# A planner's constant for one exponential, and how open feed-forward chains are completed before the last output tiles, in a fused attention and feed-forward kernel

## The chip, the cores and the metric

The kernel runs on one core of a Trainium2 chip. The metric is the device time of one execution in microseconds, less is better; the median of several runs is compared. The core has five engines with a queue each: TensorE (PE in the profile, its weight loads as PEld), VectorE (DVE), ScalarE (ACT), GpSimd (POOL) and SyncE (SP). Each works through its own list in order and waits on semaphores for the others.

## The reference

Input x has 2048 rows of 512 numbers. Two branches are computed from it and mixed by a gate for each row, all in bfloat16:

```python
g = sigmoid((x * gate_w).sum(-1, keepdims=True))
qkv = (x @ wqkv) -> q, k, v, 32 heads of 16 numbers     # a: attention
p = softmax(q @ k^T * 16 ** -0.5)                       # 32 x 2048 x 2048
a = (p @ v, heads put side by side) @ wo
b = (silu(x @ w_gate) * (x @ w_up)) @ w_down            # b: feed-forward, F = 1792
out = g * a + (1 - g) * b
```

The softmax has 32 x 2048 x 2048 exponentials, 134 million. That is the large part of the elementwise work.

## The kernel before

**Tiling.** The queries are cut into 4 blocks of 512 (qb), the heads into 8 groups of 4 (g). A unit is one (qb, g); there are 32. A unit walks over 16 tiles of 128 keys, so there are 512 slots (SLOTS), each of 4 score blocks of 128 keys x 512 queries, one for each head.

**Two ways to an exponential.** Most slots go to ScalarE: `emit_pair` puts two score blocks side by side into one PSUM tile s_t (two of them exist), and one activation writes their exponentials to e_t, 128 x 1024. The other slots go to VectorE: `emit_d` puts a score block into d_t, one of three single PSUM banks, and VectorE works out the exponential bit by bit: a first pass y_t<-d_t for each of four blocks, then passes over the whole 128 x 2048 tile (z_t by bit masks, a scaling to u_t, its square, a product with z_t), an addition that an accumulating DMA on GpSimd's queue does, and a last pass y_t<-y_t. The buffer u_t is at times a part of kaug or wd_t, and the profile then names that. `v_unit` and `v_take` decide when VectorE takes another slot, from the end of a unit backwards: it takes one when VectorE's clock in the plan leaves room and the unit's ScalarE work would not be done sooner.

**What else runs.** The probabilities are multiplied with v into o_ps (`emit_pv`), which a cast takes to osb. Beside it run the projections (kp, qp, vp), the feed-forward work, and the output. Feed-forward work comes in chains of small pieces: for each qb 14 gate/up chains (gu_a, gu_b, 8 pieces each: two matmuls a piece, then a tanh th on ScalarE and two VectorE steps gs and mt), then two down chains (dps_a, dps_b, 28 pieces each), whose results VectorE scales into bblk. The output rows of an earlier qb are made by chains a_ps. For the last qb a chain `last_pieces` of 10 pieces makes the products of the first two row tiles (a_l_a, a_l_b) without the last head group, and `tail` makes those of the other two (al).

**What sets the order.** The order of each engine's instructions is written out by a planner that runs when the program is built. It keeps clocks `plan.pe`, `plan.dve` and `plan.act` and adds fixed costs to them: 0.216 us for a matmul step, 0.6 to 1.135 us for the passes of VectorE, 0.48 us for a tanh, and ACT_US = 0.935 us for an exponential of 128 x 1024. Between two score pairs TensorE gets side work for as long as the next s_t tile is not free by these clocks:

```python
        room = s_end[pairs[0] % 2] - plan.pe      # s_end: the planned end of the exponential that frees s_t
```

`fill_dve` hands VectorE's list out up to `plan.pe`. A Pacer chooses among the chains by deadline, and deadlines are slots, not microseconds. A chain can have chains before it (`after`) and a condition (`cond`); `force(c)` puts out what is left of a chain at once, its predecessors first, and pays the VectorE work that it is owed (`owed` is the list of VectorE and other steps that are put off until their inputs are ready). The cost that the planner takes for the ScalarE part of what is left of a unit is another constant, TILE_US = 1.87, which stays.

**The end.** When all exponentials are placed, a loop places the last products with v. With one of them left it calls `tail(0)`, which places the first half of the al products; then come the last product with v, the cast to osb, the rest of al (`tail(1)`), the denominators of the last head group (dt, rt, rps), on_l, one matmul for each of four row tiles, the gate's factor, and the output. `tail(0)` needs bblk scaled for all four row tiles (`scaled`) and the head group before the last one normalised (`here_done`).

Of the kernel before, what the change touches and what calls it, by code (L numbers as in the profile page):

```python
# [78 lines left out]
def kernel(  # L79
# [76 lines left out]
    def mm(*args, **kw):  # L156
        return ordered(nc.tensor.matmul(*args, **kw))  # L157

    def act(*args, **kw):
        ordered(nc.scalar.activation(*args, **kw))  # L160
# [88 lines left out]
    for h in range(8):  # L249
        c = 2 * (h % 4) + h // 4  # L250
# [33 lines left out]
    owed = []  # L284
# [19 lines left out]
    def spend_v(cost, ready=0.0, key=None):  # L304

        if key is not None and key == plan.last:
            cost += 0.13
        plan.last = key
        plan.dve = max(plan.dve, ready) + cost

    def pay(i=0):
        ready, cost, f, c, key = owed.pop(i)
        spend_v(cost, ready, key)
        keep, plan.chain = plan.chain, None
        f()
        plan.chain = keep
        if c is not None:
            c.owed -= 1
            if c.done():
                c.done_at = plan.slot  # L320
# [27 lines left out]
    def emit_piece(c):  # L348
        mms, f = c.pieces[c.i][:2]
        c.i += 1  # L350
        keep, plan.chain = plan.chain, c
        f()
        plan.chain = keep
        if c.done():
            c.done_at = plan.slot
        return mms

    def force(c):
        for a in c.after:
            force(a)  # L360
        while not c.out():
            while c.cond is not None and not c.cond():
                if owed:
                    pay()
                else:
                    for f in at.pop(min(at)):
                        f()
            emit_piece(c)
        while c.owed:
            pay()  # L370
# [282 lines left out]
    def down_pieces(qb, tq):  # L653

        def rows(t):
            return lambda fc: (mt[:, fc, t * P:(t + 1) * P], wd_t[:, fc, :])

        def done_down(pa, pb):
            for t, p in ((tq, pa), (tq + 1, pb)):
                later(0.65, lambda t=t, p=p: end(t, p))  # L660

        def end(t, p):
            n = qb * TQ + t
            share = omg if qb < QB - 1 else ge
            vec.tensor_scalar(out=bblk[:, t, :], in0=p[:, 0:D], scalar1=share[:, n:n + 1],
                              scalar2=None, op0=ALU.mult)
            if qb == QB - 1:
                scaled.add(t)
            m_free(p, plan.dve)
        return two_banks(FC, "dps", rows(tq), rows(tq + 1), done_down)  # L670
# [27 lines left out]
    def emit_pair(bs):  # L698
# [10 lines left out]
        def exp():  # L709
            act(out=e_t[:], in_=s_t[:], func=ACT.Exp, scale=inv_sqrt_dh)  # L710
            plan.act = max(plan.act, ready) + ACT_US
            s_end[i] = plan.act + 0.2
# [5 lines left out]
        pairs[0] += 1  # L718

    exps = []  # L720
    ACT_US = 0.935

    def flush_act(before=None):

# [203 lines left out]
    def last_rows(t):  # L928
        cs = slice(t * P, (t + 1) * P)
        return lambda i: ((onc[QB - 1][:, i, cs], wo_t[:, i, :]) if i < NB - 1 else  # L930
                          (osbs[UNITS - 2][:, cs], wo_l[:, 0, :]) if i == NB - 1 else (ident[:, :], bblk[:, t, :]))
# [7 lines left out]
    def tail(k):  # L939

        if k == 0:
            assert here_done and len(scaled) == TQ
            for c in list(pace.chains):
                force(c)
            al = ps_s.tile([P, 2 * QBW], F32, tag="s", name="al")
            a_ps.extend([al[:, 0:QBW], al[:, QBW:2 * QBW]])
        todo = [(tq, i) for tq in (2, 3) for i in range(NB + 1)]
        for tq, i in todo[:5] if k == 0 else todo[5:]:
            w, r = last_rows(tq)(i)
            mm(a_ps[tq][:, 0:D], lhsT=w, rhs=r, start=(i == 0), stop=False)  # L950
# [86 lines left out]
    pace = Pacer()  # L1037
# [52 lines left out]
    for qb in range(QB):  # L1090
        a0 = f0 + per * qb
        for fc in range(FC):
# [12 lines left out]
            c = pace.add(pcs, 58, a0 + per * (0.6 if qb < QB - 1 else 0.68) * (fc + 1) / FC, prev)  # L1105
            prev = [c]
        for tq in range(0, TQ, 2):
            c = pace.add(down_pieces(qb, tq), 0 if qb else 100, a0 + per * (0.6 + 0.3 * (tq + 2) / TQ if qb < QB - 1 else 0.68 + 0.32 * (tq + 2) / TQ), prev + fin_prev + gates)
# [105 lines left out]
    def side(most):  # L1214

        due = any(not c.out() for n in range(plan.slot, plan.slot + 12) for c in need.get(n, []))
        cur = pace.cur
        begun = cur is not None and not cur.out() and cur.i and pace.credit > -3
        c = pick() if pace.credit > 0 or due or begun else None
        if c is None:  # L1220
            return None
        mms, _, takes = c.pieces[c.i][:3]
        mode, two = c.pieces[c.i][3:] or ("F", None)
        if two and two["seq"] == plan.seq:
            return None
        t = m_ready(int(takes)) if takes else 0.0
        if t is None or t > plan.pe or 0.226 * mms + (0.1 if plan.mode != mode else 0.0) > most:
            return None
        return c
# [70 lines left out]
    while au < UNITS:  # L1300
# [10 lines left out]
        if room > 0.02:  # L1311
# [6 lines left out]
            c = side(room + SLACK)  # L1318
# [26 lines left out]
    while closed < UNITS or vops or added or vcur:  # L1345
        fill_dve()
        while owed and owed[0][0] <= plan.pe:
            pay()
        if plan.slot < SLOTS + 1:
            begin(plan.slot + 1)  # L1350
            pace.credit = max(pace.credit, 2.0)
        if vcur:
            emit_d()
            continue
        c = side(2.0)
        if not pv_list(plan.pe) and c is not None:
            put_piece(c)
            continue
        if closed == UNITS - 1 and pvs[closed] == KT - 1:
            tail(0)  # L1360
        next_pv()
# [13 lines left out]
    un = UNITS - 1  # L1375
    osb = osbs[un]
    tail(1)
    dt = m_tile("dt")
    for tq in range(TQ):
# [54 lines left out]
```

## Time and profile before

| | |
|---|---|
| median of 4 runs | 844.99 us (843.76 to 846.82) |
| profiled execution | 845.75 us, span of the trace 844.0 us |
| mean granted TensorE clock | 0.996 |
| busy: PE, DVE, ACT, POOL | 91%, 94%, 97%, 11% of the span |
| exponentials on ScalarE (e_t) | 846, busy 792.4 us |
| slots on VectorE (z_t) | 89 |
| tanh (th) | 56, busy 37.9 us |

The span goes from the first to the last instruction of the trace; the execution's own time holds 1.75 us more. A group's line reads: kernel line, engine, operation, output<-input by the program's names, sizes, count | busy us, mean ns of one | idle time of the engine ahead of it, and what ended that. Line 160 is the helper through which all activations go, 157 that of the matmuls, 166 that of VectorE's instructions, so groups are told apart by their tiles. A wait's line reads: who waited <- who released it: us in total, times, longest. Neighbouring instructions of one engine overlap a little, so the mean duration of one is longer than the step from one start to the next.

### The profile page before, as it was taken

What the parts mean: (1) busy time and instruction counts of PE and PEld (TensorE: products, weight loads), DVE (VectorE), ACT (ScalarE), POOL (GpSimd) and SP (SyncE); (2) the same over time, 40 slices, a digit from 0 to 9 for tenths busy, and PEclk for the clock granted to TensorE, in tenths of its full rate; (3) what the DMA queues carried; (4) which work ended last, traced back from release to release, by engine and by line L of the source; (5) the groups of instructions that cost most, each with busy time, mean ns of one, the idle gap of its engine ahead of it and who ended that gap; (6) DMA issues with size and microseconds to landing.
All of it is one profiled execution on the core that took longest, in us unless ns stands there. A gap on an engine that the chain in (4) does not pass through costs nothing.

```text
span 844.0 us, 16253 instructions
## 1 busy us (share of the span) xinstructions
PE 769.0 (91%) x6076; PEld 263.5 (31%) x6076; DVE 796.6 (94%) x1159; ACT 815.6 (97%) x912; POOL 93.2 (11%) x122
## 2 busy tenths in 40 slices
PE   7999998999888998889889989899899898988997
PEld 3222233332232332222223333223333233332332
DVE  6999998999999999999999999999998999999996
ACT  3999999999999999999999999999999999999996
POOL 5010100010011011011010100100100110111000
PEclk9999999999999999999999999999999999999999
DMA  9432445345454334554444354454442454354232
GB/s 205 127 65 49 85 80 113 64 93 109 95 107 99 74 70 104 108 115 91 87 94 90 70 113 95 84 121 85 104 84 55 91 122 94 77 116 98 57 69 50
DMA packets 101415, 78.23 MB, mean 93 GB/s; under 512 B 77760, under 2 KB 89624, under 8 KB 101336
## 3 DMA queue, kind: packets, MB, share of 16 engines
q0 software_dynamic: 12672, 46.14, 28.7%
q1 hardware_dynamic: 86792, 30.60, 15.3%
q8 instruction: 47, 0.77, 0.4%
q10 hardware_dynamic: 1872, 0.46, 0.2%
q14 instruction: 32, 0.26, 0.1%
HBM read 20.83 MB, written 2.34 MB: 27 GB/s over the span
## 4 chain that ended last, share of the span: by engine, by line
DVE 25%; PE 14%; ACT 7%; issue 3%; DMA 1%; SPq 0%; DVEq 0%; ACTq 0%
DVE y_t L166 9%; ACT e_t L160 7%; DVE kaug L166 4%; PE s_t L157 4%; DVE u_t L166 4%; PE o_ps L157 2%; DVE z_t L166 2%; DVE gs L166 2%; PE dps_b L157 2%; DVE mt L166 2%; PE d_t L157 1%; PE dps_a L157 1%; PE gu_b L157 1%; PE gu_a L157 1%; DVE osb L166 1%
## 5 line engine op out<-in xcount | busy, mean ns | idle before, releaser
L160 ACT ACTIVATE e_t<-s_t 128x1024 bf16<-128x1024 f32 x846 | 792.4, 1105 | 8.8 <-PE s_t L157 7.2
L157 PE MATMUL s_t<-qx,kaug 64*128 64x512 bf16 x1376 | 294.3, 381 | 33.8 <-ACT e_t L160 29.0
L166 DVE TENSOR_SCALAR y_t<-d_t 128x512 uint16<-128x512 f32 x356 | 234.7, 682 | 16.8 <-PE d_t L157 13.7
L157 PEld LDWEIGHTS <-kaug 64*128 64x128 bf16 x2048 | 137.3, 93 | 322.5 <-issue 286.9
L157 PE MATMUL o_ps<-e_t,vaug 128*32 128x512 bf16 x1692 | 160.0, 390 | 1.4 <-DVE osb L166 1.0
L157 PE MATMUL gu_a<-xT,wg 64*128 64x512 bf16 x448 | 137.0, 380 | 0.0
L157 PE MATMUL gu_b<-xT,wu 64*128 64x512 bf16 x448 | 135.7, 380 | 1.2 <-DVE y_t L166 0.9
L157 PE MATMUL d_t<-qx,kaug 64*128 64x512 bf16 x288 | 107.5, 378 | 16.0 <-DVE y_t L166 8.5
L157 PEld LDWEIGHTS <-vaug 128*32 128x32 bf16 (+1 forms) x2132 | 45.7, 94 | 146.3 <-issue 144.8
L778 POOL DMA_DIRECT2D y_t<-u_t x44 | 40.2, 913 | 351.0 <-PE s_t L157 192.9
L778 POOL DMA_DIRECT2D y_t<-kaug x38 | 35.9, 946 | 311.7 <-PE s_t L157 161.6
L157 PE MATMUL dps_a<-wd_t,mt 64*128 64x512 bf16 x224 | 65.3, 376 | 0.0
L157 PE MATMUL dps_b<-wd_t,mt 64*128 64x512 bf16 x224 | 65.0, 376 | 0.3 <-DVE y_t L166 0.2
L166 DVE TENSOR_SCALAR z_t<-y_t 128x2048 uint16<-128x2048 uint16 x89 | 61.5, 691 | 2.1
L166 DVE TENSOR_SCALAR y_t<-y_t 128x2048 uint16<-128x2048 uint16 x89 | 60.9, 684 | 1.5 <-DMA y_t<-u_t 1.1
L166 DVE TENSOR_TENSOR u_t<-u_t 128x2048 f16<-128x2048 f16 x44 | 53.8, 1223 | 1.1
L166 DVE TENSOR_TENSOR u_t<-u_t,z_t 128x2048 f16<-128x2048 f16 x44 | 53.5, 1217 | 0.1
L157 PE MATMUL s_t<-q,kaug 64*128 64x512 bf16 x212 | 44.0, 386 | 7.6 <-ACT e_t L160 7.0
L166 DVE TENSOR_TENSOR kaug<-kaug 128x2048 f16<-128x2048 f16 x39 | 47.7, 1223 | 0.9
L157 PEld LDWEIGHTS <-wg 64*128 64x128 bf16 x448 | 41.4, 95 | 20.5 <-issue 8.5
L166 DVE TENSOR_TENSOR kaug<-kaug,z_t 128x2048 f16<-128x2048 f16 x39 | 47.5, 1217 | 0.1
L157 PEld LDWEIGHTS <-wu 64*128 64x128 bf16 x448 | 42.2, 95 | 16.6 <-issue 1.5
(131 smaller groups left out, 636.5 us busy)
## 6 DMA issues: line engine op xcount, KB each, us to landing
y_t<-u_t POOLq DMA_DIRECT2D x44, 512.0 KB, 4.8
y_t<-kaug POOLq DMA_DIRECT2D x38, 512.0 KB, 4.8
wg<-in_B_w_gate_dram SPq DMA_DIRECT2D x56, 128.0 KB
wu<-in_B_w_up_dram SPq DMA_DIRECT2D x56, 128.0 KB
y_t<-wd_t POOLq DMA_DIRECT2D x6, 512.0 KB, 4.7
on<-osb SPq DMA_DIRECT2D x120, 16.0 KB
rb<-rr SPq DMA_DIRECT2D x15, 128.0 KB
wd_t<-in_B_w_down_dram SPq DMA_DIRECT2D x7, 256.0 KB
```

What stands on the lines that cost most here:

```text
L157: return ordered(nc.tensor.matmul(*args, **kw))
L160: ordered(nc.scalar.activation(*args, **kw))
L166: return lambda *a, **kw: ordered(f(*a, **kw))
L778: nc.gpsimd.dma_start(out=ya, in_=ua, accum_op=ALU.add)
```

## The change

The planner counts 0.920 us instead of 0.935 us for an exponential. And `tail(0)` first completes all chains that are open, in the order of their deadlines, then pays all steps that are still owed, and only then makes sure of its conditions; before, it made sure of them first, and completed open chains in the order in which they were added.

```diff
@@ -718,7 +718,7 @@
         pairs[0] += 1
 
     exps = []
-    ACT_US = 0.935
+    ACT_US = 0.92
 
     def flush_act(before=None):
 
@@ -939,9 +939,11 @@
     def tail(k):
 
         if k == 0:
+            for c in sorted(pace.chains, key=lambda c: c.deadline):
+                force(c)
+            while owed:
+                pay()
             assert here_done and len(scaled) == TQ
-            for c in list(pace.chains):
-                force(c)
             al = ps_s.tile([P, 2 * QBW], F32, tag="s", name="al")
             a_ps.extend([al[:, 0:QBW], al[:, QBW:2 * QBW]])
         todo = [(tq, i) for tq in (2, 3) for i in range(NB + 1)]
```

## The prediction

> **What bounds the kernel now.** I read, in this order, the engine table and the chain of waits of the page, the list of waits, ScalarE's instructions in order of time, the groups by cost, and the last 20 us of the timeline.
>
> ```profile
> span 844.0 us, 16253 instructions
> PE 769.0 (91%) x6076; PEld 263.5 (31%) x6076; DVE 796.6 (94%) x1159; ACT 815.6 (97%) x912; POOL 93.2 (11%) x122
> ...
> DVE 25%; PE 14%; ACT 7%; issue 3%; DMA 1%; SPq 0%; DVEq 0%; ACTq 0%
> ```
>
> The table alone would name ScalarE, at 97%. The chain does not: ScalarE carries 7 points of it, VectorE 25, TensorE 14. Three engines are almost full, and the two that look less full are the ones that release the work that ended last.
>
> ```profile
> PE s_t L157 <- ACT e_t L160: 36.7, 109, 0.9
> ...
> DVE y_t L166 <- PE d_t L157: 13.7, 23, 1.0
> ...
> PE d_t L157 <- DVE y_t L166: 9.6, 21, 0.9
> ...
> ACT e_t L160 <- PE s_t L157: 7.2, 15, 1.5
> ```
>
> Here each engine waits for another. ScalarE seems to lose 7.2 us only, but a delay shorter than the overlap of two exponentials leaves no idle time in this view. Their spacing does show it. First come all exponentials, from the view of tile e_t, then two stretches of ScalarE's timeline that hold nothing but exponentials (start, length, count).
>
> ```profile
> L160 ACT ACTIVATE e_t<-s_t x846: 1018/1112/1312, 18.7 to 834.5; 128x1024 bf16<-128x1024 f32 x170
> ```
>
> ```profile
> 298.75 13.86 ACT L160 ACTIVATE e_t<-s_t 128x1024 bf16<-128x1024 f32 x15 [0.17 <-PE s_t L157]
> ...
> 815.38 20.27 ACT L160 ACTIVATE e_t<-s_t 128x1024 bf16<-128x1024 f32 x22 [0.75 <-PE s_t L157]
> ```
>
> From first start to last start is 815.8 us. The 56 tanh take 0.47 us each in this order (one starts at 312.35, the next exponential at 312.82), 26.3 us in all, so one of the 845 steps took (815.8 - 26.3) / 845 = 0.934 us. Undisturbed it takes (20.27 - 1.11) / 21 = 0.912 us, and (13.86 - 1.11) / 14 = 0.911 us. So ScalarE is kept waiting for about 845 x 0.022 = 18.6 us, most of it hidden. The kernel runs at the pace for which its instruction order was written (0.935), and ScalarE is a little faster than that. That is the room this change can use.
>
> One rule of the Trainium skill says there is no such room. The page "ScalarE: Activation LUTs", section "What ACT_TABLE_LOAD costs", gives 186 ns + 0.833 ns per element for an activation and an overlap of about 93 ns between neighbours; for 1024 elements that is an estimate of 0.946 us per exponential, and ScalarE would be the bound with nothing to recover. The 0.912 above differs, and it decides; by the page the sum would be that of the first rival below.
>
> **Part 1: 0.935 becomes 0.920.** No instruction is made faster. The number moves the planner's clock: it thinks that each of 846 exponentials ends 0.015 us earlier, 12.7 us in all. Fewer microseconds between two score pairs mean less VectorE work fits, and VectorE decides how many key tiles it takes over. One such tile costs, from the groups:
>
> ```profile
> L166 DVE TENSOR_SCALAR y_t<-d_t 128x512 uint16<-128x512 f32 x356 | 234.7, 682 | 16.8 <-PE d_t L157 13.7 <-PE s_t L157 2.0 <-PE gu_a L157 0.7
> ...
> L166 DVE TENSOR_SCALAR z_t<-y_t 128x2048 uint16<-128x2048 uint16 x89 | 61.5, 691 | 2.1
> L166 DVE TENSOR_SCALAR y_t<-y_t 128x2048 uint16<-128x2048 uint16 x89 | 60.9, 684 | 1.5 <-DMA y_t<-u_t 1.1 <-DMA y_t<-kaug 0.2
> ```
>
> To these 357.1 us come the same table's three other passes, each spread over the buffers u_t, kaug and wd_t: scaling 31.2 + 27.8 + 4.1, squares 53.8 + 47.7 + 7.3, products 53.5 + 47.5 + 7.3. That is 637.3 us for 89 tiles, 7.16 us a tile. If m tiles go back to ScalarE, the planner's time shrinks by 12.7 - 1.84 m (two exponentials a tile), and VectorE, equally full in a shorter time, must lose as much: 7.16 m = 12.7 - 1.84 m, m = 1.4. So I expect 1 or 2 tiles fewer of 89, and about 3 exponentials more than 846. With them:
> - VectorE loses 1.4 x 7.16 = 10.1 us of work.
> - ScalarE gains 2.8 x 0.934 = 2.6 us.
> - TensorE: a tile on VectorE has four score matmuls one after the other (some 0.21 us apart in the timeline), a pair for ScalarE two side by side. So it loses about 1.4 x 2 x 0.21 = 0.6 us.
> - Each lost tile takes away its accumulating transfer on POOL's queue (512 KB). POOL is busy for 11%, so I cost that at nothing; were it needed, the addition lands after 4.8 us. The weight loads on SP's queue keep their number and order; they move with the feed-forward chains, two chains ahead of use.
>
> What of it is on the path? The chain weighs the engines 25 : 14 : 7, that is 0.54, 0.30 and 0.15 of the 46 points that are engine work. -10.1 x 0.54 - 0.6 x 0.30 + 2.6 x 0.15 = -5.3 us. The ends: -10.1 if the whole shorter order comes true, +2.6 if ScalarE is the sole pace. I take -5.3, since all three engines have holes and none of them alone sets the time. What is late next is ScalarE: the shorter order and its 2.6 us of new work leave it 5.9 us of its 18.6 us (18.6 - 10.1 - 2.6) if all comes true, so holes cannot vanish much further.
>
> **Part 2: completion at the end.** The order shrinks, but the feed-forward work doesn't, and it shares PSUM banks and VectorE's evictions with everything else. So it ends later against the last exponential. Before, it just gets done:
>
> ```profile
> 827.31 0.74 DVE L166 TENSOR_SCALAR bblk<-dps_b,ge 128x512 bf16<-128x512 f32 x1
> ...
> 831.63 0.38 PE L157 MATMUL a_l_a<-bblk,ident 64*128 64x512 bf16 x1
> ...
> 833.87 0.39 PE L157 MATMUL s_t<-qx,kaug 64*128 64x512 bf16 x2 [0.53 <-ACT e_t L160]
> ...
> 835.96 0.40 PE L157 MATMUL o_ps<-e_t,vaug 128*32 128x512 bf16 x4
> 836.41 0.69 DVE L166 CAST osb<-o_ps 128x512 bf16<-128x512 f32 x1 [2.04 <-PE o_ps L157]
> ```
>
> The last down products are scaled at 827.31 to 828.05, the output pieces a_l end at 832.0, the last exponential starts at 834.5. From 831.9 to 834.8 TensorE is busy for 2.15 of 2.90 us; by start spacing it issues 3 score pairs and 3 groups of o_ps, about 6 x 0.22 = 1.3 us. So its cover is 0.75 to 1.6 us. Each quarter of the feed-forward work belongs to a quarter of the order; a quarter of 10.1 is 2.5 us of lateness, if the earlier quarters catch up. Over the cover it sticks out by 0.9 to 1.75 us. I take 1.0. In that case chains are open at the tail, and they are completed ahead of the al products and the last group of o_ps on TensorE; behind that group wait, one after the other, the osb cast, the denominators dt and rps, on_l, four output products, mt and the output's transfer (835.96 to 844.0), so each microsecond there is one of the end. On VectorE the owed scalings stand ahead of that cast. The ends of this term: 0, and 8.5 if all 10.1 us of lateness is left at the end.
>
> **Sum.** The profiled execution took 845.75 us (span 844.0 and 1.75 around it); 845.75 - 5.3 + 1.0 = 841.45. It stands 0.76 above the median of 844.99, so I forecast 840.7 for the median, -0.5%.
>
> **Rivals.** (1) *ScalarE is the pace*: the holes stay as they are, because they come from matmuls that sit in TensorE's order between two score pairs, and there are 3 exponentials more: +2.6, and the tail's 1.0. 844.99 + 3.6 = 848.6, slower. For it: 97% busy, and TensorE's longest list of waits (36.7 us) ends on ScalarE. Against it: the 0.022 us a step, and its small part in the chain. It decides from the point at which less than 1.1 us of the 18.6 us is won back (3.6 less 2.5, the 0.3% at which a measurement of this kernel can tell a change from none). (2) *The feed-forward work is the pace at the end*: about 6 us of the lateness piles up there instead of 2.5, as one chain of down products is 28 steps of two matmuls, 6 us at 0.21 each. -5.3 + 6 - 1.6 = -0.9: 844.1, within 0.3%. For it: PE is full in the last 20 us with these very steps. At over 9.4 us open (1.6 + 5.3 + 2.5) it would be slower. (3) *The constant does too little*: the order absorbs the 12.7 us in gaps that the planner leaves on TensorE and VectorE (47 us of VectorE idle in the span), no tile moves: 845.0.
>
> **How the numbers follow.** Forecast 0.52, rival 1 0.22, rival 2 0.18, rival 3 0.08. Faster by over 0.3%: 0.48 of the forecast (the rest of it is too small a gain) and 0.04 of rival 2, 0.52. Within: 0.04 + 0.10 + 0.08 = 0.22. Slower: 0.22 + 0.04 = 0.26. The range goes from the whole shorter order with nothing at the tail, 844.99 - 10.1 = 834.9, to rival 1's 848.6; the likeliest case alone has 835 to 842.5.
>
> **What would show it.** Right: 86 to 88 z_t instructions instead of 89, 848 to 852 exponentials, a mean step nearer 0.92 than 0.934, VectorE's busy time down by about 10 us, a_l pieces that end less than 1 us ahead of the last exponential or behind it, and the distance from the last exponential's start to the span's end, 9.5 us now, at 10 to 11. Wrong: a step still at 0.93 (rival 1), that last distance at over 14 us (rival 2), 89 tiles and the same order (rival 3).

## The result, and the profile after

The changed kernel takes 847.68 us (median of 47 runs), the kernel before 844.85 (71 runs): ratio 1.003, 95% interval 1.002 to 1.004. It is slower by 2.8 us; 840.7 was forecast, a gain. The profiled execution took 850.90 us with a span of 847.4.

The same parts of the page, from the changed kernel:

```profile
span 847.4 us, 16311 instructions
PE 774.3 (91%) x6104; PEld 267.0 (32%) x6104; DVE 788.6 (93%) x1149; ACT 814.8 (96%) x914; POOL 90.4 (11%) x122
...
DVE 23%; ACT 16%; PE 16%; issue 4%; DMA 2%; DVEq 0%; ACTq 0%
```

VectorE works 8.0 us less (796.6 to 788.6), and ScalarE's part in the chain goes from 7 to 16. Next the tile views of z_t and e_t (count: shortest/median/longest in ns, first to last start):

```profile
L166 DVE TENSOR_SCALAR z_t<-y_t x88: 627/693/695, 29.0 to 821.7; 128x2048 uint16<-128x2048 uint16 x88
```

```profile
L160 ACT ACTIVATE e_t<-s_t x848: 1017/1151/1315, 18.9 to 832.4; 128x1024 bf16<-128x1024 f32 x170
```

One slot went back to ScalarE, two exponentials more, and yet the last one starts at 832.4 instead of 834.5. A step is (832.40 - 18.94 - 56 x 0.47) / 847 = 0.929 us, against 0.934. So the loop became 2.1 us shorter in this execution. The end became longer: from the last exponential's start to the end of the span it is 15.0 us, against 9.6. That is +5.4 - 2.1 = +3.4 us of span (rounded), 844.0 to 847.4. The timeline of the end shows on what TensorE spends it:

```profile
834.47 0.38 PE L157 MATMUL dps_a<-wd_t,mt 64*128 64x512 bf16 x1
...
834.89 0.75 DVE L166 TENSOR_SCALAR bblk<-dps_a,ge 128x512 bf16<-128x512 f32 x1 [2.38 <-PE dps_b L157]
...
835.69 0.37 PE L157 MATMUL a_l_b<-wo_t,on 64*128 64x512 bf16 x1 [0.62 <-DVE bblk L166]
...
837.88 0.38 PE L157 MATMUL a_l_a<-bblk,ident 64*128 64x512 bf16 x1
...
839.38 0.40 PE L157 MATMUL o_ps<-e_t,vaug 128*32 128x512 bf16 x4
...
839.83 0.69 DVE L166 CAST osb<-o_ps 128x512 bf16<-128x512 f32 x1 [3.53 <-PE o_ps L157]
```

Before, the last down products were scaled at 827.31 and the a_l pieces done at 832.0, ahead of the last exponential. Now 8 steps of dps and all 10 of a_l come after it, with a wait of 0.62 us for bblk. Only behind them stand the al products and the last group of o_ps, and the cast waits 3.53 us for that group. It starts 7.0 us after the last exponential's start (839.4 - 832.4), against 1.5 before (835.96 - 834.48). The rest of the end is the same.

### The profile page after: what moved, and what is told of

It reads as the page before. It is cut to its first block, busy times and chain, and to the rows that moved or that the text cites. A ratio compares the mean times of both kernels' runs of the same rounds, so it can differ in the third digit from the quotient of the medians.

```text
span 847.4 us, 16311 instructions
## 1 busy us (share of the span) xinstructions
PE 774.3 (91%) x6104; PEld 267.0 (32%) x6104; DVE 788.6 (93%) x1149; ACT 814.8 (96%) x914; POOL 90.4 (11%) x122
## 4 chain that ended last, share of the span: by engine, by line
DVE 23%; ACT 16%; PE 16%; issue 4%; DMA 2%; DVEq 0%; ACTq 0%
ACT e_t L160 15%; DVE y_t L166 8%; PE s_t L157 5%; DVE u_t L166 4%; DVE kaug L166 4%; PE o_ps L157 3%; PE dps_a L157 2%; DVE z_t L166 2%; DVE mt L166 2%; PE d_t L157 2%; DVE gs L166 2%; ACT th L160 1%; PE dps_b L157 1%; DMA y_t<-kaug 1%; PE gu_a L157 1%
## 5 line engine op out<-in xcount | busy, mean ns | idle before, releaser
L157 PE MATMUL s_t<-qx,kaug 64*128 64x512 bf16 x1380 | 284.4, 384 | 46.8 <-ACT e_t L160 41.7
L157 PEld LDWEIGHTS <-kaug 64*128 64x128 bf16 x2048 | 141.1, 93 | 334.2 <-issue 298.8
L166 DVE TENSOR_SCALAR y_t<-d_t 128x512 uint16<-128x512 f32 x352 | 231.7, 682 | 12.3 <-PE d_t L157 10.6
L157 PE MATMUL gu_a<-xT,wg 64*128 64x512 bf16 x448 | 134.7, 376 | 0.0
L778 POOL DMA_DIRECT2D y_t<-kaug x37 | 33.5, 905 | 310.9 <-PE s_t L157 139.7
L166 DVE TENSOR_TENSOR kaug<-kaug 128x2048 f16<-128x2048 f16 x37 | 45.3, 1224 | 1.1
L166 DVE TENSOR_TENSOR kaug<-kaug,z_t 128x2048 f16<-128x2048 f16 x37 | 45.0, 1217 | 0.0
```

The costliest lines, as they stand in the source:

```text
L166: return lambda *a, **kw: ordered(f(*a, **kw))
L778: nc.gpsimd.dma_start(out=ya, in_=ua, accum_op=ALU.add)
```

## The experiments

Theory A: the loop wins, and the open feed-forward work at the end takes more than that. Theory B: ScalarE is the pace, and its additional exponentials are the loss. The first four runs separate them; later ones are on other constants and on the clock. All times are medians, and each ratio is to the kernel before in the same call, whose median went from 844.65 to 845.31. "Half clock" is how long TensorE's granted clock was 0.5 before the last exponential, in the profiled execution.

| run | constant | what else | exponentials | last one starts | from there to the end | half clock | time, us | ratio to before (95%) |
|---|---|---|---|---|---|---|---|---|
| before | 0.935 | | 846 | 834.5 | 9.6 | 6.8 | 844.85 | |
| change | 0.920 | | 848 | 832.4 | 15.0 | 17.0 | 847.68 | 1.002 to 1.004 |
| e1 | 0.935 | last down chain held back | 846 | 834.7 | 15.6 | 13.6 | 852.07 | 1.006 to 1.010 |
| e2 | 0.920 | deadlines 8 slots earlier | 850 | 833.3 | 9.6 | 13.6 | 842.02 | 0.994 to 0.997 |
| e3 | 0.920 | the change again | 848 | 832.3 | 15.1 | 17.0 | 847.74 | 1.001 to 1.005 |
| e4 | 0.935 | deadlines 8 earlier | 848 | 837.2 | 9.9 | 10.2 | 847.70 | 1.001 to 1.004 |
| e5 | 0.920 | 8 earlier, more filler | 850 | 828.1 | 10.8 | 3.4 | 840.66 | 0.993 to 0.997 |
| e6 | 0.900 | 8 earlier | 854 | 833.9 | 14.1 | 3.4 | 849.76 | 1.004 to 1.008 |
| e7 | 0.930 | | 848 | 830.8 | 9.5 | 3.4 | 841.73 | 0.995 to 0.997 |
| e8 | 0.920 | 4 earlier | 852 | 832.6 | 9.5 | 10.2 | 842.67 | 0.996 to 0.998 |
| e9 | 0.920 | more filler | 848 | 830.2 | 11.6 | 6.8 | 843.72 | 0.997 to 0.999 |
| e10 | 0.930 | more filler | 848 | 832.2 | 9.6 | 3.4 | 843.88 | 0.997 to 1.000 |
| e11 | 0.935 | more filler | 846 | 832.5 | 11.9 | 3.4 | 846.89 | 1.001 to 1.005 |
| e12 | 0.920 | open steps left out | 848 | 829.4 | 11.3 | 3.4 | 843.50 | 0.9960 to 1.0005 |

**e1, the end alone.**

```diff
-            c = pace.add(down_pieces(qb, tq), 0 if qb else 100, ...
+            c = pace.add(down_pieces(qb, tq), (507 if qb == QB - 1 and tq else 0) if qb else 100, ...
```

> The constant is 0.935 as before; only the second down chain of the last query block is held back until slot 507, so that feed-forward work is open when the exponentials end (some 11 down pieces and all 10 pieces of a_l). Theory A, the open feed-forward work at the end is what the change costs (the last exponential's start to the end of the span went from 9.5 to 15.0 us): 846 or so exponentials as before, last exponential at 833 to 835 us, that distance 15 to 16 us, time 849 to 851 us. Theory B, ScalarE's pace with its extra exponentials is the cost and the end is hidden: no slower than before, 844 to 846 us.

852.07 us. The loop is that of before (846 exponentials, the last at 834.7), the end is 6.1 us longer, the time 6.8 us above that of before in the same call (845.31). Open work at the end costs what theory A says, with the old constant. The time lies above the 849 to 851 that were expected, though the parts came as expected: 834.7 + 15.6 + 1.75 = 852.1, more than the range that was put on their sum. The loop took as long as before although half clock was 13.6 us and not 6.8, so the price of half clock that e12 gives is not seen in this pair of profiles.

**e2 and e4, feed-forward work earlier, with the new constant and the old.**

```diff
-    f0, f1 = 72, SLOTS - 8
+    f0, f1 = 64, SLOTS - 8
```

> The change with its constant 0.920, but the feed-forward deadlines start 8 slots earlier (64 for 72), so that nothing of the last down chain is open when the exponentials end. Theory A: the distance from the last exponential's start to the end falls back to 9.5 to 10.5 us and the loop keeps what it won, 841 to 843 us, faster than before by 2 to 4 us. Theory B: the distance shrinks but the exponentials end later by as much, 847 to 849 us.

> The control of the earlier feed-forward deadlines: 64 for 72 with the constant 0.935 of the kernel before. Theory A: the end was already covered there, so nothing is won, 844 to 846 us. If the earlier deadlines by themselves make the kernel faster, 842 to 843 us, then the gain of the run with 0.920 says nothing on the constant.

With 0.920 it is 842.02 us, faster than before by 3.3 us, and the end is 9.6 us again. The same shift with 0.935 is slower than before by 2.4 us: no gain comes from the deadlines themselves at that constant. (That order has one slot fewer on VectorE and a step of 0.935 us, with the end covered; its time lies above both ranges that were expected.) Theory B is out: e2 has 4 exponentials more than the kernel before, and wins. From e2, the a_l pieces and the last o_ps:

```profile
833.34 0.39 PE L157 MATMUL a_l_a<-bblk,ident 64*128 64x512 bf16 x1
...
834.84 0.40 PE L157 MATMUL o_ps<-e_t,vaug 128*32 128x512 bf16 x4
```

The last group of o_ps starts 1.5 us after the last exponential's start at 833.3, as before; one pair of steps of a_l is left open there, not eighteen steps.

**e3, the change again.**

> The changed kernel once more, for a second profile and as the reference of this call. Both theories: 847 to 849 us. A third theory, that the first profile was a poor execution (granted clock 0.990 against 0.996): last exponential's start earlier than the 832.4 us of the first profile by 1 to 3 us, the distance to the end 15.0 us as before.

847.74 us, the last exponential at 832.3, the end 15.1 us. The two profiles agree; the third theory, a poor first profile, is not supported by that. Both hold the same four phases of half clock at the same places, and both took longer (850.90 and 849.11 us) than the median of 847.7, at a granted clock of 0.990 where the median is 0.992.

**e8, another shift.**

```diff
-    f0, f1 = 72, SLOTS - 8
+    f0, f1 = 68, SLOTS - 8
```

> The change with 0.920 and feed-forward deadlines 4 slots earlier instead of 8, another order of about the same kind (2 more exponentials, nothing open at the end). Theory A: distance to the end 9.5 to 10.5 us and 842 to 844.5 us. If the gain with 8 slots was one lucky order: 845 to 848 us with that distance just as short.

842.67 us with the end covered: e2 was no single lucky order. Orders differ by some microseconds all the same, with one constant and the end covered in both: e4 and the kernel before by 2.4 us, e7 and e10 by 2.2 us.

**e6 and e7, other constants.**

```diff
-    ACT_US = 0.92
+    ACT_US = 0.9      # e6, with f0 = 64; e7: 0.93, with f0 = 72
```

> The constant at 0.900, below ScalarE's undisturbed step of 0.904 to 0.912 us, feed-forward deadlines 8 slots earlier; some exponentials more (about 854). Theory A, ScalarE's own pace and its waits are a floor and the loop follows the planner only in part: step 0.922 to 0.930 us, last exponential at 833 to 838 us, distance to the end 10 to 13 us as the a_l pieces are open again, time 844 to 850 us. Rival, the loop follows the planner's clock at a third or more, as from 0.935 to 0.920: step 0.920 or less, last exponential at 828 to 831, time 839 to 842 us.

> The change with 0.930 in place of 0.920; nothing else. Its order leaves no feed-forward work open at the end, so the new completion in tail does nothing. Theory A: the loop wins a third of what it wins with 0.920 and the end is covered: distance to the end 9.5 to 10.5 us, 843 to 845 us, same or faster by up to 2 us. If a smaller constant were bad by itself: 846 to 848 us.

0.930 is 3.3 us faster than before (844.99 to 841.73), more than expected, with nothing open at the end. 0.900 is 4.8 us slower: its step of 0.925 us is no shorter than the 0.922 to 0.928 us of the other orders with 0.920, while 8 exponentials more than before and 14.1 us at the end are to be paid. The step of e7 (0.9275 us) lies among them too, so below 0.930 these runs show no clear gain in the step from a smaller constant.

**e5, e9, e10, e11, the filler.** A filler is a step of four matmuls that adds zeros to o_ps when little is planned on TensorE. The threshold rises:

```diff
-                    w for t, w in work_at[-24:] if t > plan.pe - 3.0) < 6.5:
+                    w for t, w in work_at[-24:] if t > plan.pe - 3.0) < 7.5:
```

> The run with 0.920 and feed-forward deadlines 8 slots earlier, plus more filler matmuls: a filler is placed on TensorE when fewer than 7.5 matmul steps (6.5 before) were planned for the last 3 us. Theory: the half-clock phases of TensorE (granted clock 0.990 in that run, four phases) keep ScalarE waiting some 1.2 us each; with fewer of them the step from exponential to exponential falls from 0.928 to about 0.925 us and the time by 1 to 3 us, to 839 to 841. Rival, these phases cost nothing that matters or are not set by the work ahead of them: 842 to 843 us, clock 0.990 as in that run.

> The change (0.920, deadlines as in the change) with one number beside it: a filler matmul is placed when fewer than 7.5 steps (6.5 before) were planned for the last 3 us. The other order leaves only about half of the a_l pieces open at the end, where the change leaves 8 steps of dps and all 10 of a_l. Theory A: distance from the last exponential's start to the end 10.5 to 12 us (15.0 in the change), half-clock time of TensorE at most 7 us (17 in the change), last exponential at 828 to 831 us, time 840 to 843 us. Rival, the constant 0.920 loses with these deadlines whatever the tail holds: 846 us or more.

> 0.930 with the same filler threshold of 7.5, deadlines unchanged, nothing open at the end: a candidate for the best. Theory: distance to the end 9.5 to 10 us, last exponential at 829 to 831 us, 840 to 842 us. Rival, the filler costs TensorE's time where no half-clock phase is avoided: 842 to 844 us.

> The control of the filler threshold: 7.5 with the constant 0.935 of before. This order leaves all 10 a_l pieces open at the end. Theory A: distance to the end 12 to 13 us (9.6 before), last exponential at 832 to 834 us with fewer half-clock phases, 845 to 847 us. Rival, the filler by itself makes the gain: 840 to 842 us.

On e2 (e5) the half clock goes from 13.6 to 3.4 us and the time to 840.66, the best version found: 0.995 of before, 0.993 to 0.997. On the change itself (e9) only a_l pieces are still open, the end is 11.6 us and the time 843.72, faster than before with the change's own constant and deadlines. With 0.930 (e10) it is no gain: 843.88, above the range expected and above e7, which had but one phase of 3.4 us to lose. With 0.935 (e11) the filler's order leaves the 10 a_l pieces open (end 11.9 us), and it is slower than before by 2 us. So filler alone does not make the gain. Where half clock fell, the last exponential came earlier: by 5.2 us for 10.2 us less of it (e5 against e2), by 2.2 for 10.2 (e9 against the change), by 2.0 for 3.4 (e11 against before). The filler also reshuffles the order, so these three give no clean price.

**e12, the change's own order without the open steps.**

```diff
+                left_out = au >= UNITS and k > 0 and not (stop and k == 2 * n - 1)
                 ...
                     rows = slice(64 * h, 64 * h + 64)
+                    if left_out:
+                        continue
```

> The change with its very order, but 16 of the 18 feed-forward and output steps that are open when the exponentials end are left out (7 of 8 of the last dps chain, 9 of 10 of a_l; so part of the last output rows is not computed). Theory A: these steps are the loss at the end, 16 x 0.216 = 3.5 us plus the wait of 0.6 us for bblk: distance from the last exponential's start to the end 10.5 to 12 us (15.0 in the change), time 842.5 to 844.5 us (847.7 in the change). Rival, the end is bound by something else that stands beside them: distance over 13 us, 846 to 848 us. Where the loop itself ends must stay as it is: last exponential at 832 to 833 us.

843.50 us, 4.2 below the change (the kernel before differs by 0.2 between the two calls), and the end falls from 15.0 to 11.3 us: 16 steps at 0.216 us are 3.5 of these 3.7 us. What is left above 9.6 is the last dps step, the scalings and their wait. The one thing that missed is the loop. Its order is the change's but for the steps left out, yet the last exponential starts at 829.4, not 832.4:

```profile
L160 ACT ACTIVATE e_t<-s_t x848: 1017/1144/1315, 18.7 to 829.4; 128x1024 bf16<-128x1024 f32 x170
```

The granted clock tells the two apart. The windows of the changed kernel (the number behind the POOL column is the mean granted clock):

```profile
20.00:30.00 10.00, 8.36 (x44) 1.92 (x43) 7.22 (x12) 7.48 (x8) 0.00 (x0) 0.83 0.60 146
145.00:165.00 20.00, 18.52 (x137) 5.34 (x132) 15.88 (x26) 18.36 (x21) 1.86 (x2) 0.83 0.58 116
355.00:365.00 10.00, 8.65 (x64) 2.74 (x60) 9.18 (x14) 9.27 (x11) 0.86 (x1) 0.83 0.42 86
555.00:565.00 10.00, 8.42 (x56) 2.43 (x56) 9.83 (x15) 9.49 (x11) 1.91 (x2) 0.83 0.73 136
```

and the same windows of e12, with the one in which its only phase lies:

```profile
20.00:30.00 10.00, 8.24 (x52) 2.49 (x51) 8.35 (x14) 8.45 (x10) 0.00 (x0) 1.00 0.65 174
145.00:165.00 20.00, 17.77 (x143) 6.08 (x142) 16.62 (x26) 20.00 (x24) 1.86 (x2) 1.00 0.58 123
355.00:365.00 10.00, 9.81 (x84) 3.65 (x82) 9.86 (x15) 10.00 (x12) 0.00 (x0) 1.00 0.39 88
555.00:565.00 10.00, 9.19 (x73) 2.81 (x73) 9.72 (x15) 9.89 (x11) 1.83 (x2) 1.00 0.45 91
725.00:740.00 15.00, 13.49 (x98) 4.75 (x95) 13.46 (x20) 13.84 (x16) 2.03 (x2) 0.89 0.50 94
```

At half clock for 3.4 of 10 us the mean is 0.83, so the change had 3.4 + 6.8 + 3.4 + 3.4 = 17.0 us of it and e12 3.4. ScalarE is busy for 18.36 of the 20 us from 145 to 165 in the one and for all 20 in the other. Its timeline in the change shows how a phase acts, the scores coming late:

```profile
148.37 4.80 ACT L160 ACTIVATE e_t<-s_t 128x1024 bf16<-128x1024 f32 x5
154.00 2.12 ACT L160 ACTIVATE e_t<-s_t 128x1024 bf16<-128x1024 f32 x2 [0.84 <-PE s_t L157]
156.61 1.02 ACT L160 ACTIVATE e_t<-s_t 128x1024 bf16<-128x1024 f32 x1 [0.49 <-PE s_t L157]
```

13.6 us less at half clock came with a last exponential 3.0 us earlier, 0.22 us for each. As the order is the same, the n-th exponentials can be set side by side. e12's lead grows by 1.2, 2.2, 1.2 and 0.3 us at the four phases of the change, 0.29 us for each of half clock, and falls by 1.6 us at its own phase; another 0.9 us it loses near 680 us, where neither is at half clock. The timed runs say the same for whole executions: over the 47 runs of the change, span against time at half clock (2 x (1 - clock) x span) has a slope of 0.33 us per us, correlation 0.95, and the line meets full clock at a span of 841.5; 29 runs of before have slope 0.34 and meet it at 841.2. The fastest run of the change had a clock of 0.999 and 843.85 us, the slowest 0.988 and 852.03. Its median clock is 0.992 and that of before 0.996 to 0.997.

## Why the prediction was wrong

**Part 1, the order shrinks: right in direction and size, in part by luck.** 1.4 slots were forecast to go back, 1 did (88 z_t, 848 exponentials); 10.1 us less VectorE work, it is 8.0. For the loop -5.3 us was taken. In the profiled execution it is -2.1, with 17.0 us of half clock against 6.8 before. In e12, the same order with 3.4 us of it, it is -5.1 (834.5 to 829.4). At the half clock of before and 0.33 us for each, that is -2.1 - 0.33 x 10.2 = -5.5 by the one and -5.1 + 0.33 x 3.4 = -4.0 by the other. That the weights of the chain give this size is not shown to be more than luck: e7, with a third of the step in the constant, gives back the same one slot and has a loop 3.6 us shorter (834.5 to 830.8) at 3.4 us less of half clock. One reading was off: a fed step was taken as 0.912 us, but in the trace of before the median step from start to start is 0.904 us. ScalarE's waits were then 845 x 0.030 = 25 us and not 18.6; no term of the sum hangs on that.

**Part 2, the end: the step that failed.** The text took 2.5 us of lateness for the feed-forward work, "if the earlier quarters catch up", less what is covered, and put down 1.0 us at the end; +5.4 was measured. In the text's own terms the lateness is 8.4 us, from 2.5 us ahead of the last exponential's start to 5.9 behind it, and cover took 3.0 of it where the text had 0.75 to 1.6. The views of gu_a, the first part of this work, and of the last steps of a_l, before and in the changed kernel:

```profile
L157 PE MATMUL gu_a<-xT,wg x448: 372/376/632, 132.5 to 789.5; 64*128 64x512 bf16 x150
L157 PE MATMUL a_l_a<-bblk,ident x2: 375/376/376, 828.8 to 831.6; 64*128 64x512 bf16 x2
```

```profile
L157 PE MATMUL gu_a<-xT,wg x448: 373/376/631, 141.9 to 801.0; 64*128 64x512 bf16 x150
L157 PE MATMUL dps_a<-wd_t,mt x224: 373/376/387, 279.6 to 834.5; 64*128 64x512 bf16 x112
L157 PE MATMUL a_l_a<-bblk,ident x2: 376/376/376, 836.4 to 837.9; 64*128 64x512 bf16 x2
```

and the last steps of a_l in e7, whose last exponential starts at 830.8:

```profile
L157 PE MATMUL a_l_a<-bblk,ident x2: 376/376/376, 822.6 to 825.2; 64*128 64x512 bf16 x2
```

Before, dps_a ended at 826.2. The starts of gu_a and of e_t, sorted by time, give the place of each of the four blocks of queries in the order:

| run | first gu_a of each block, us | exponentials started by then | by the last gu_a | end of a_l, seen from the last exponential's start |
|---|---|---|---|---|
| before | 132.5, 309.2, 482.6, 655.7 | 121, 304, 482, 662 | 798 | 2.5 us ahead |
| change | 141.9, 312.6, 491.6, 667.0 | 131, 306, 492, 675 | 814 | 5.9 us behind |
| e12 | 140.5, 308.9, 486.7, 661.8 | 131, 306, 492, 675 | 814 | (left out) |
| e7 | 132.4, 301.7, 476.2, 651.2 | 120, 296, 478, 660 | 796 | 5.3 us ahead |
| e11 | 132.8, 308.6, 483.0, 657.2 | 121, 304, 485, 664 | 804 | 2.7 us behind |

So the lateness is not what the text made of it, an equal share from each quarter as the order shrinks. The first block is 9.4 us late already, at a point by which an order 10.1 us shorter has shrunk by 10.1 x 132.5 / 844 = 1.6 us. The second is 3.4 us late, so 6.0 us are caught up; the third and the fourth, with 9.0 and 11.3 us, lose them again. Counted in exponentials the change has its blocks 10, 2, 10 and 13 later, and e12 has the same counts with 13.6 us less of half clock: the lateness is in the order that the planner wrote. It does not follow from a shorter order alone, either. In e7 the order is shorter, and its feed-forward work is done further ahead of the end than before; in e11 the constant is the old one, only the filler and the tail differ from before, and all 10 steps of a_l are open. Why the planner places the blocks so late with 0.920 was not tested and stays open. What the open steps cost is shown by e12 (16 of them left out, 3.7 us less at the end), and that starting the work earlier removes them by e2 and e8.

Rival 2 had the open work at the end as the loss, with 6 us and a chance of 0.18. With the 8.5 that the term named as its own end, the sum is -5.3 + 8.5 = +3.2, slower than before. That this stands near the measured +2.8 is luck: the end cost 5.4, and the clock's share is not in it. The text kept that end out of the forecast on an assumption that no row of the profile supported. In the trace of before the dps matmuls run from 274.6 to 305.6, 451.2 to 480.8, 620.8 to 652.4 and 793.6 to 826.2 us, each stretch 4 to 6 us behind the last gu_a of its block, and the next block's gu_a starts 2 to 4 us behind them: a stream without a long pause.

**The clock: not in the sum at all.** Before had two phases of half clock, and the prediction has no term for them. The change's order gets more (median clock 0.992 for 0.9965), 2 x 0.0045 x 846 = 7.6 us more at half clock, at 0.33 us each 2.5 us. The two lines above meet full clock at 841.5 and 841.2, so without half clock the change would be 0.3 us slower, the longer end of 5.4 us and a loop about 5.1 us shorter; with the clock's 2.5 that makes the +2.8 that was measured. Against the -4.3 of the forecast, 7.1 us are missing: 4.4 at the end, 2.5 by the clock, the rest in the loop. That the order is the cause of the lower clock is shown by the medians of the same two kernels in several calls (0.992 twice and 0.993 in e12 for the change's order, 0.996 to 0.997 in four for before); which of its gaps sets a phase off stays open.

**The rivals.** Rival 1 is refuted by e2, and by a loop that ended 2.1 us earlier with two exponentials more. Its sign, "a step still at 0.93", is met by the profile's 0.929 all the same; the sign was too coarse, and e12's step for this order is 0.926. Rival 3 is refuted by the 848 exponentials. The sign that the text gave for rival 2, over 14 us from the last exponential to the end, is what the profile shows (15.0). The change's second part would have nothing to complete in the order of before, where no step is open. No run has 0.920 with the old tail, and none puts the open steps behind the last group of o_ps, so what the second part costs or saves by itself is not measured.

## What to carry to other kernels

When a constant makes a planner write another order, do not scale the end with the constant: of three orders with the same deadlines, 0.930 covered its end better than 0.935 and 0.920 left 18 steps open. The order is fixed when the program is built, so the steps that stand behind the last exponential can be counted in it; each costs its length at the end once the cover is used up, and that work has to be started earlier (e2, e8) before the shorter order pays. Take the pessimistic end of such a term unless a row speaks for less. Read the granted clock as a term of the sum: compare kernels at like clock, and look at several executions before a microsecond in one profile is explained.

## What the runs showed of the hardware

A phase at half clock lasted 3.4 us or 6.8 us, and came with TensorE at 91% busy over the span. In the change no gap between its matmuls was longer than 0.90 us from 25 us to 830 us, and three of its four phases begin in that stretch. Half clock cost the kernel a fifth to a third of its length (0.22 between two profiles of one order, 0.33 over 47 runs), single phases between a tenth and a half. The Trainium skill, page "TensorE: Matmul & The Clock Gate", section "Part 1: The HAM clock gate (the "warmup" mystery)", describes a clock that is either half or full and is judged on free-running windows of about 3.4 us. The phases here agree with both numbers. On the window the runs are divided: the same loop order had 17.0 us in one execution and 3.4 in another, which fits a window that is not tied to the kernel's start, but the two profiles of the change have their four phases at the same places.

ScalarE's step, when fed, was 0.904 us for 1024 elements from PSUM: that is the median from start to start in the trace of before (0.912 over the stretch of 22 that the prediction took). The skill's page "ScalarE: Activation LUTs", section "What ACT_TABLE_LOAD costs", gave the estimate of 0.946 us, which the measurement does not bear out. Another page, "Perfetto Trace Analysis", section "Optimizing Scalar/DVE Operations", has about 51 ns of access overhead for ScalarE on PSUM, which with 0.833 ns an element makes an estimate of 0.904 us; the measurement agrees with that. The constant of 0.900, below the measured step, did not make the loop follow (e6).
